# Linear attention and a two-layer MLP on one core: a new order of the first six microseconds' work on TensorE

## The chip, the cores and the metric

The kernel runs on one core of a Trainium2 chip. The metric is the device time of one launch in microseconds (us), taken as the median of several runs. The engines are TensorE (PE in the profile, PEld for its weight loads), VectorE (DVE), ScalarE (ACT), GpSimd (POOL) and SyncE (SP). Each plays its own list of instructions in order, and waits for the others by semaphores. Only PE writes products; they land in PSUM, which has 8 banks, and DVE or ACT bring them to SBUF.

## The reference

Inputs are r, k, v of shape (4 batches, 8 heads, 768 tokens, 48), a decay w and a bonus u of shape (8, 48), and two weight matrices of 384 x 2048 and 2048 x 384. Cut to what is computed:

```python
for t in range(S):                       # linear attention with a decaying state
    cur = einsum('bhd,bhe->bhde', u * k[t], v[t])
    y[t] = einsum('bhd,bhde->bhe', r[t], state + cur)
    state = w * state + einsum('bhd,bhe->bhde', k[t], v[t])
x = y.transpose(0, 2, 1, 3).reshape(3072, 384)
h = x @ w_in                             # MLP
out = maximum(0.01 * h, h) @ w_out
```

## The kernel before, in words

The tokens are cut into 24 stages of 128 (6 per batch). Within a stage the decay is split around the middle token, so that a stage's attention becomes matrix products: q~ = r times a table of powers of w, k~ = k times the inverse powers. The tables (`qtab`, `ktab`, L297 and L298) are exponentials of ln w, which is spread over all partitions by one product of a row of ones with the row w (L294) on PE and a logarithm on ACT (L296).

A stage n goes through steps, each a letter in the string ORDER (L26): **P** makes q~ and k~ on DVE (L322, L324); **T** turns both by products with an identity matrix (`ident`), in two halves of four products (L367), each half copied out of PSUM (ACT L378; the first k~ half on DVE, L375); **A** makes the scores k~ q~ (L391); **M** masks them with a triangle on DVE (L409); **X** multiplies the turned q~ and k~ on DVE (L329), and **K** makes from it the diagonal's sums and the new k v products on PE (L421, L425, L430); **Q** scales v by these sums on DVE (L337); **S** makes the next state on DVE (L475); **Y** puts the attention's output together on PE (L508, L513) with a copy on ACT (L528); **G** and **J** are the first MLP product on PE with its activation on ACT (L541 and L558), **H** the second (L575). **U** spreads u. From stage 8 on the turning is done by a DMA (L317) instead of T.

Three steps occur at the head alone. **C** (`decay_columns`, L449 and L450) makes columns of w and of w times u, by sixteen products with one column each from single rows; ACT takes the logarithm of the w columns (L457) and DVE copies the w\*u columns into `wu` (L459), which K uses. **W** (L466) makes from the logarithms the state's decay `wl` on ACT. **F**n (`fill`, L249) issues n products of 128x512 from a tile of ones (L254) whose result nobody reads. `fill(EARLY)` stands ahead of the w product (L294).

The order is written out by hand: the string ORDER is walked letter by letter, and each step appends its instructions to the lists of the engines it uses. So the order of the letters is the order on every engine. A helper records for each instruction what it reads and writes and gives it the waits that follow from that. After ORDER a loop takes the remaining stages in pairs.

POOL issues nearly all loads (L217 for r, k and v of one stage, L227 for a quarter of w_in, L231 for a quarter of w_out), in the order of the string LOADS (L25); `id` and `tri` in it are the two small tiles `ident` (L262) and `mask` (L266), made by POOL itself from the ones. r and k of stage 0 come by SP and ACT (L205), v of stage 0 is issued by POOL ahead of LOADS. The stages' loads land one after the other until about 48 us.

Of the kernel before, what the change touches and what calls it, by code (L numbers as in the profile page):

```python
# [20 lines left out]
NFB = DFF // 128  # L21
NSL = HD // 128

FIRST, EARLY = 6, 2
LOADS = """r1 k1 r2 k2 wi0 id v1 r3 tri k3 v2 wi1 k4 r4 v3 wi2 k5 r5 r6 k6 v4 v5 k7 wi3 r7 v6 v7 wo3 wo2 wo1 wo0"""  # L25
ORDER = """  # L26
C W P0 P1 F1 T0 T1 P2 A0 X0 M0 A1 K0 T2 Q0 X1 Y0 A2 S0 M1 K1 X2 G0.0 Q1 P3 S1 Y1 T3 K2 M2 G1.0 X3 A3 U G0.1 S2 G1.1 Q2 M3 Y2 K3 P4
T4 Q3 G2.0 G2.1 G0.2 S3 G2.2 G1.2 Y3 P5 A4 P6 X4 M4 T5 X5 G3.0 K4 Q4 A5 S4 T6 G3.1 K5 G3.2 Y4 M5 L8 Q5 Y5 P7 A6 G1.3 J2.0 J2.1 T7
M6 X6 X7 K6 J2.2 J2.3 A7 S6 J2.4 J2.5 L9 Q6 G2.3 G0.3 J2.6 M7 L10 J2.7 L11 G3.3 K7 S7 P8 Q7 Q8 P9 H0 Q9 K8 H1 P10 L12 K9 H2 S8 S9
Y6 Y7 A8 A9 P11 M8 H3 M9 L13  # L30
# [90 lines left out]
def bass_rwkv5_eagle__then__act_leaky_relu_kernel(  # L121
# [146 lines left out]

    for name in LOADS.split():
        if name == "id":  # L270
# [547 lines left out]
```

## Time and profile before

| what | value |
|---|---|
| time, median of 3 runs (lowest to highest) | 170.77 us (170.43 to 171.89) |
| the profiled run, its own time | 171.27 us |
| span of the profiled run, first to last instruction | 169.5 us |
| PE busy | 163.1 us, 96% of the span |
| DVE, ACT, POOL busy | 114.9, 93.3, 103.8 us |
| DVE idle from 9.79 us to 18.36 us | 0.26 and 1.14 us |
| first turning on PE | 7.30 us |
| first mask on DVE | 10.13 us |

The profile is of one execution. A group's line gives line, engine, operation, what it writes and reads, its count, busy time and mean length, and then the idle time of the engine just before such instructions. In the timeline a row gives the start from the span's begin, the length of the merged instructions, and, in brackets, how long the engine had been idle before and what ended that. PE's products are pipelined: the next starts before the one before has ended, so distances from start to start tell its speed better than lengths.

### The profile page before, as it was taken

To read this page: it belongs to the slowest core of one execution; us is meant where nothing else is said; L and a number is where in the kernel's file an instruction comes from. 1 tells how busy PE (TensorE), PEld (TensorE's weight loads), DVE (VectorE), ACT (ScalarE), POOL (GpSimd) and SP (SyncE) were. 2 spreads that over 40 slices of the span, in tenths; PEclk is the share of its full clock that TensorE was granted. 3 is DMA by queue.
4 is the path that set the end of the run, shared out by engine and by line. 5 is a ranking of instruction groups with operands and counts; after the bars stand their busy time and mean duration, and the time that the engine had idled before them with its cause. 6 is when DMAs were issued, how large, how long until landed. Compare 5 with 4: busy or idle time off the path is not lost.

```text
span 169.5 us, 5112 instructions
## 1 busy us (share of the span) xinstructions
PE 163.1 (96%) x2203; PEld 129.1 (76%) x2203; DVE 114.9 (68%) x211; ACT 93.3 (55%) x176; POOL 103.8 (61%) x117
## 2 busy tenths in 40 slices
PE   6799999999999999999999999999999999999992
PEld 1577898889656876876866867867867899898991
DVE  7699766752998869379289299099199976053272
ACT  4752888789122852842933934824834836829320
POOL 7999999990379799791992995974506500000000
PEclk9999999999999999999999999999999999999999
DMA  5999999999999989999699499599107102011032
GB/s 95 117 155 159 170 155 171 194 185 145 126 167 197 167 50 126 214 73 114 172 74 156 130 74 154 135 106 205 51 0 173 48 4 93 4 40 55 4 115 70
DMA packets 99258, 19.66 MB, mean 116 GB/s; under 512 B 92322, under 2 KB 99236, under 8 KB 99236
## 3 DMA queue, kind: packets, MB, share of 16 engines
q0 software_dynamic: 76512, 10.03, 90.9%
q1 hardware_dynamic: 21682, 9.11, 25.6%
q8 instruction: 17, 0.28, 0.7%
q10 hardware_dynamic: 1042, 0.20, 0.6%
q14 instruction: 5, 0.04, 0.1%
HBM read 20.45 MB, written 4.72 MB: 148 GB/s over the span
## 4 chain that ended last, share of the span: by engine, by line
PE 93%; POOL 4%; ACT 1%; issue 1%; DVE 0%; DVEq 0%; POOLq 0%
PE ps_all L558 31%; PE ps_all L575 25%; PE ps_all L639 11%; PE ps_all L541 7%; PE ps_all L508 7%; PE ps_all L391 4%; PE ps_all L367 3%; PE ps_all L425 3%; POOL rk_sb L217 2%; PE ps_all L513 1%; ACT tp L378 1%; POOL v_sb L217 1%; PE ps_all L430 1%; PE ps_all L421 1%; POOL w_in_sb L227 0%
## 5 line engine op out<-in xcount | busy, mean ns | idle before, releaser
L558 PE MATMUL ps_all<-xT,w_in_sb 128*128 128x256 bf16 x480 | 54.5, 273 | 0.0
L354 POOL TENSOR_TENSOR at<-ident,s_tok 128x512 bf16<-128x512 bf16 x32 | 35.0, 1121 | 29.0 <-DVE s_tok L346 29.0
L558 PEld LDWEIGHTS ps_all<-xT,w_in_sb 128*128 128x128 bf16 x480 | 46.7, 98 | 6.1
L564 ACT ACTIVATE gT<-ps_all 128x512 bf16<-128x512 f32 x80 | 47.7, 597 | 5.8 <-PE ps_all L558 1.2
L575 PE MATMUL ps_all<-w_out_sb,gT 128*128 128x384 bf16 x256 | 43.3, 326 | 0.0
L575 PEld LDWEIGHTS ps_all<-w_out_sb,gT 128*128 128x128 bf16 x256 | 24.4, 98 | 15.9
L401 DVE CAST_PREDICATED at<-mask,ps_all 128x1024 bf16<-128x1024 uint16 x16 | 18.8, 1219 | 20.6 <-PE ps_all L391 20.6
L581 ACT ACTIVATE out_sb<-ps_all 128x384 f32<-128x384 f32 x16 | 7.8, 490 | 38.4 <-PE ps_all L575 38.4
L217 POOL DMA_DIRECT2D v_sb<-in_v_dram x24 | 22.6, 945 | 0.4 <-issue 0.4
L217 POOL DMA_DIRECT2D rk_sb<-in_k_dram x23 | 21.6, 941 | 0.0
L217 POOL DMA_DIRECT2D rk_sb<-in_r_dram x23 | 21.3, 929 | 0.0
L670 DVE TENSOR_TENSOR out_sb<-ps_all,snap 128x192 f32<-128x192 f32 x13 | 4.4, 355 | 15.1 <-PE ps_all L639 14.5
L344 DVE TENSOR_TENSOR rku<-rk_sb,ku 128x384 bf16<-128x384 bf16 x16 | 13.8, 861 | 0.6
L528 ACT ACTIVATE xT<-ps_all 128x384 bf16<-128x384 f32 x24 | 11.0, 490 | 5.1 <-PE ps_all L508 3.0
L541 PE MATMUL ps_all<-xT,w_in_sb 128*128 128x128 bf16 x192 | 13.0, 225 | 0.0
L541 PEld LDWEIGHTS ps_all<-xT,w_in_sb 128*128 128x128 bf16 x192 | 11.8, 101 | 0.5 <-issue 0.3
L409 DVE TENSOR_TENSOR at<-ps_all,mask 128x512 bf16<-128x512 f32 x16 | 10.2, 682 | 2.2 <-PE ps_all L391 2.2
L546 ACT ACTIVATE gT<-ps_all 128x512 bf16<-128x512 f32 x16 | 9.6, 599 | 3.8 <-PE ps_all L541 3.1
L508 PE MATMUL ps_all<-at,v_sb 128*32 128x128 bf16 x384 | 11.4, 228 | 0.0
L378 ACT ACTIVATE tp<-ps_all 128x512 bf16<-128x512 f32 x15 | 8.2, 596 | 3.7 <-PE ps_all L367 3.7
L508 PEld LDWEIGHTS ps_all<-at,v_sb 128*32 128x32 bf16 x384 | 8.4, 99 | 2.2 <-issue 0.5
L508 PE MATMUL ps_all<-tp,st 128*32 128x128 bf16 x240 | 9.8, 223 | 0.0
(80 smaller groups left out, 197.2 us busy)
## 6 DMA issues: line engine op xcount, KB each, us to landing
out_dram<-out_sb SPq DMA_DIRECT2D x22, 192.0 KB, 2.6
v_sb<-in_v_dram POOLq DMA_DIRECT2D x24, 96.0 KB, 5.5
rk_sb<-in_r_dram POOLq DMA_DIRECT2D x23, 96.0 KB, 5.2
rk_sb<-in_k_dram POOLq DMA_DIRECT2D x23, 96.0 KB, 4.6
w_in_sb<-in_moe_w_in_dram POOLq DMA_DIRECT2D x4, 384.0 KB, 7.0
w_out_sb<-in_moe_w_out_dram POOLq DMA_DIRECT2D x4, 384.0 KB, 10.9
out_dram<-out_sb SPq DMA_DIRECT2D x4, 96.0 KB, 1.7
tp<-qk SPq DMA_TRANSPOSE x16, 4.4
```

What stands on the lines that cost most here:

```text
L217: add("pool", lambda: G.dma_start(dst, src), R=pace, W=[key], dma=f"{which}{n}")
L344: add("dve", lambda: V.tensor_tensor(rku[i2][:, :], r_of(n), ku[i2][:, :], ALU.mult), R=[("r", n % NRK), ("ku", i2)], W=[("rku", i2)])
L354: add("pool", lambda hh=hh, s_of=s_of: G.tensor_tensor(at[ia][:, hh, :, :], ident[:, :].unsqueeze(1).to_broadcast([128, NP, 128]), s_of.un ...
L401: add("dve", lambda: V.copy_predicated(at[n % NAT][:, :, :, :].rearrange("p two m i -> p (two m) i"), mask[:, :].bitcast(mybir.dt.uint16). ...
L409: add("dve", lambda hh=hh, part=part: V.tensor_tensor(at[n % NAT][:, hh, :, :], part, mask[:, :].unsqueeze(1).to_broadcast([128, NP, 128]) ...
L508: last = PE.matmul(ps_y[32 * q:32 * q + 32, 128 * s:128 * s + 128], a, m, start=first_mm and (s == 0 or n >= DIAG), stop=last_mm and n >= ...
L528: add("act", lambda: A.activation(xT[m % NX][:, :, 128 * half:128 * half + 128], ps_y[:, 0:HD].rearrange("p (s t) -> p s t", t=128), AF.Copy),
L541: last = PE.matmul(ps_g[:, 128 * f:128 * f + 128], w_in_sb[:, s, 128 * fb:128 * fb + 128], xT[ix][:, s, t], start=s == 0, stop=s == NSL - 1)
L558: last = PE.matmul(ps_g[:, 256 * f:256 * f + 256], w_in_sb[:, s, 128 * fb:128 * fb + 128], xT[ix][:, s, :], start=s == 0, stop=s == NSL - 1)
L564: add("act", lambda: A.activation(gT[ig][:, 2 * j:2 * j + 2, :].rearrange("p f t -> p (f t)"), ps_g[:, :], AF.Prelu, alpha=0.01), R=[key], ...
L575: last = PE.matmul(ps_o[:, 0:HD], gT[ig][:, s, 128 * half:128 * half + 128], w_out_sb[:, s, :], start=s == 0, stop=s == NFB - 1)
L639: done = PE.matmul(ps_o[:, 0:NH], lhs[:, s, :], rhs[:, s, :], start=first and s == 0, stop=s == HF - 1, skip_group_check=not (first and last))
```

## The change

Four things in the two strings and one constant:

- EARLY goes from 2 to 3: three dummies instead of two ahead of the w product.
- In ORDER, P0 (q~ and k~ of stage 0), a group of five dummies, P1 and the first turning T0 now come ahead of C and W; before, C and W came first, with one dummy and both turnings behind. A group of two dummies stands between W and T1. On DVE this puts q~ and k~ of stages 0 and 1, and the copy of the first turned k~, ahead of the two w\*u copies; on ACT it puts the copy of the first turned q~ ahead of the logarithms of the columns and the state's decay. On PE the sixteen one-column products move behind the first turning.
- In LOADS, `id` moves from behind the first quarter of w_in to the front: POOL makes `ident` right behind its first issue (v of stage 0), ahead of the loads of r and k of stages 1 and 2 and of w_in's first quarter.
- Everything from P2 on, and the rest of LOADS from v1 on, keeps its order.

```diff
-FIRST, EARLY = 6, 2
-LOADS = """r1 k1 r2 k2 wi0 id v1 r3 tri k3 v2 wi1 k4 r4 v3 wi2 k5 r5 r6 k6 v4 v5 k7 wi3 r7 v6 v7 wo3 wo2 wo1 wo0"""
+FIRST, EARLY = 6, 3
+LOADS = """id r1 k1 r2 k2 wi0 v1 r3 tri k3 v2 wi1 k4 r4 v3 wi2 k5 r5 r6 k6 v4 v5 k7 wi3 r7 v6 v7 wo3 wo2 wo1 wo0"""
 ORDER = """
-C W P0 P1 F1 T0 T1 P2 A0 X0 M0 A1 K0 T2 Q0 X1 Y0 A2 S0 M1 K1 X2 G0.0 Q1 P3 S1 Y1 T3 K2 M2 G1.0 X3 A3 U G0.1 S2 G1.1 Q2 M3 Y2 K3 P4
+P0 F5 P1 T0 C W F2 T1 P2 A0 X0 M0 A1 K0 T2 Q0 X1 Y0 A2 S0 M1 K1 X2 G0.0 Q1 P3 S1 Y1 T3 K2 M2 G1.0 X3 A3 U G0.1 S2 G1.1 Q2 M3 Y2 K3 P4
```

## The prediction

> **What bounds the kernel now.** I read the page first: shares, slices, and the chain that ended last.
>
> ```profile
> span 169.5 us, 5112 instructions
> ...
> PE 163.1 (96%) x2203; PEld 129.1 (76%) x2203; DVE 114.9 (68%) x211; ACT 93.3 (55%) x176; POOL 103.8 (61%) x117
> ...
> PE   6799999999999999999999999999999999999992
> ...
> PEclk9999999999999999999999999999999999999999
> ...
> PE 93%; POOL 4%; ACT 1%; issue 1%; DVE 0%; DVEq 0%; POOLq 0%
> ```
>
> TensorE (PE) is full from the second slice on and is 93% of the chain. So whatever the head wins or loses on PE by about 20 us goes straight to the end, unless something later makes PE wait. The PEclk row says full clock throughout, which the durations contradict. The timeline of the first 22 us (start, length, engine, line, out<-in, count, idle before) shows it:
>
> ```profile
> 2.61 1.64 PE L294 MATMUL ps_all<-w_row,one_row 1*128 1x384 f32 x2
> ...
> 5.66 0.61 PE L254 MATMUL ps_all<-ones 128*128 128x512 bf16 x1
> ...
> 6.16 0.35 DVE L459 CAST wu<-ps_all 48x4 bf16<-48x4 f32 x2 [1.27 <-ACT wcol L457]
> ...
> 6.54 0.56 DVE L322 TENSOR_TENSOR qk<-r_f,tab 128x384 bf16<-128x384 f32 x1
> 6.68 0.57 POOL L262 TENSOR_SCALAR_AFFINE_SELECT ident<-ones 128x128 bf16<-128x128 bf16 x1
> ...
> 7.30 1.98 PE L367 MATMUL ps_all<-ident,qk 128*128 128x128 bf16 x16 [1.04 <-POOL ident L262]
> ...
> 9.52 0.36 DVE L324 TENSOR_TENSOR qk<-rk_sb,tab 128x384 bf16<-128x384 bf16 x1 [0.19 <-DMA rk_sb<-in_k_dram]
> ...
> 9.79 0.42 DVE L329 TENSOR_TENSOR prod<-tp 128x512 bf16<-128x512 bf16 x1
> ...
> 10.99 1.05 PE L367 MATMUL ps_all<-ident,qk 128*128 128x128 bf16 x8
> ...
> 14.21 1.49 PE L541 MATMUL ps_all<-xT,w_in_sb 128*128 128x128 bf16 x12
> ...
> 14.46 0.56 DVE L337 TENSOR_TENSOR vs<-v_sb,ps_all 128x384 bf16<-128x384 bf16 x1 [0.26 <-PE ps_all L430]
> ...
> 16.65 0.61 PE L367 MATMUL ps_all<-ident,qk 128*128 128x128 bf16 x8
> ...
> 17.53 0.83 PE L541 MATMUL ps_all<-xT,w_in_sb 128*128 128x128 bf16 x12
> ...
> 18.36 0.42 DVE L329 TENSOR_TENSOR prod<-tp 128x512 bf16<-128x512 bf16 x1 [1.14 <-ACT tp L378]
> ```
>
> Three things are to be seen. Twelve L541 products take 1.49 us at 14.21 and 0.83 us at 17.53, and eight turnings 1.05 us at 10.99 and 0.61 at 16.65: up to about 16 us PE runs at half speed. VectorE (DVE) is the second full engine there: by the busy times of the stretches 8 to 16 us it works 7.37 of 8 us, PE 7.8. And at 9.52 DVE waits for the DMA that brings k of stage 2; X0 (9.79) and the mask M0 (10.13) follow at once.
>
> **The change, step by step.** All sums are against the profiled run: 171.27 us, that is the span of 169.5 and 1.8 around it. The median of the three timed runs, 170.77, is 0.5 lower.
>
> *A third early dummy.* Dummies on PE start 0.42 us apart (two in 1.03, each 0.61 long). Three from 1.65 leave PE free at 2.91; the w product, which started at 2.61, is 0.30 later. ScalarE's ln and two exponentials follow it: the q table ends at 5.79 instead of 5.49, the k table at 6.30 instead of 6.00.
>
> *The first q~ ahead of the w\*u copies.* q~0 started at 6.54, behind the copies, with its table ready at 5.49. Now it starts at 5.84 and ends at 6.40: 0.70 earlier; its r landed at 4.7 (issued 1.19, 3.5 to landing). k~0 (needs the k table) runs 6.32 to 6.96.
>
> *ident first on POOL.* It moves from 6.68 to 2.47, behind the first v load, and is done at 3.04, so it no longer holds the first turning T0 (1.04 idle at 7.30). Four load issues (r1, k1, r2, k2) and w_in's first move 0.52 us later (its slot: 6.68 to 7.20); later issues stay. Cost between 0 and 0.52. For 0 speak the landings: the first v load lands 4.5 us after issue, the next three 4.2, 4.1 and 3.9, so they queue behind each other and an issue half a microsecond later still finds its predecessor in transfer. k2 took 4.4, and wi0 6.0. I take 0; the other end is a rival below.
>
> *Five dummies to the turning.* From the w product's start to the first one-column product was 1.57 us, so F5 starts at 2.91 + 1.57 = 4.48, runs 5 x 0.42 and ends at 6.58. q~0 is ready at 6.40, so T0 starts at 6.58, not 7.30, and PE has no hole from 1.65 to T0's end at 7.43 (two halves of 0.42 from rows of half speed).
>
> *One-column products, two dummies, then T1.* These now stand between T0 and T1. At half speed: C 1.48 (4.18 to 5.66), F2 0.84, so T1 starts at 9.75 instead of 8.25. At full speed no row shows C; its bounds are 0.74 (half) and 1.48 (nothing gained), and the nearest rows, four L421 products of two columns (0.13 us to the next start at 10.58, 0.10 at 17.10), give 1.1. With T0's second half at 7.02 to 7.24 (k~0's end), C to 8.35, F2 0.43 and T1 0.45, A0 starts at 9.3, as before (9.22). The wu copies wait for C and then stand ahead of q~2 on DVE, done by about 9.1; the state's wl, behind them on ScalarE, is not used before 12.1. k~2 still waits for its load at 9.49. So **M0 stays at 10.13** and the 0.7 won on q~0 is worth nothing: the load is late next.
>
> *So all hangs on when PE becomes fast.* In the run before, PE was occupied from 1.65 to 6.27 with holes of about 0.1, but 1.5 us of this were one-column products and 1.6 the one-row product; it stayed slow. In the change 5.8 us are occupied, 1.4 of them by the one-row product, and no one-column product among them. I take it that this makes PE fast between 5 and 8 us. [...]
>
> *What a fast PE is worth.* Not half of its 7.8 busy microseconds, since DVE's work from M0 on is the same. From 9.79 to X3 (18.36) DVE idles 0.26 and 1.14, 1.40 in all: the most that can go. I follow the chain: v·s of stage 1 (L337) starts without its 0.26, ends at 14.76 instead of 15.02; Y1 starts some 0.2 later, at 14.96. From Y's start to ScalarE's copy of it: 0.88 at full speed (20.51 to 21.39), 1.22 here; from that copy, with the two copies of T3, to X3: 1.51 (16.85 to 18.36). X3 at 14.96 + 0.88 + 1.51 = 17.35, so **1.0 earlier**; ScalarE is late next. The masks M2 and M3, Y2 and the PE-bound rest follow. Later slack: r6 lands at 24.4 for an X4 at 25.0 whose mask waits 1.32 for PE; the two DMA turnings that A8 and A9 (51.63) need land at 49.8 and 50.9, which leaves 0.7, and they are issued earlier when PE is. I take the 1.0 whole: 171.27 - 1.0 = **170.3**; the bounds are 0.5 and 1.4, so 169.9 to 170.8.
>
> **Rivals.**
> - *PE isn't fast early; slower.* [...] Then the added dummies only stand in the way: A0 comes 0.97 after T1's start, at 10.72 instead of 9.22, its mask at 11.37 instead of 10.13, 1.24 late. Of A0's 1.5 the weight loads' hole of 0.47 ahead of A1 takes some. Price 1.0 to 1.24 if PE turns fast about where it did, 0.4 if earlier, up to 1.7 if later: 171.7 to 173.0, about 172.4. [...] It decides if PE is still slow at T1.
> - *The loads move.* PE is fast, but ident's 0.52 goes through to k2 (9.49 to 10.0) and the queue behind it. M0 is 0.52 late and half of the gain is gone: 170.8, to 171.3 if the DMA turnings are late as well.
> - *PE's full gain.* If DVE's order doesn't hold PE up, 7.8 us at the ratio 0.83/1.49 give back up to 3.4: 168 to 169. Against it: DVE has no hole from 9.79 to 14.2.
>
> **How the numbers follow.** The forecast 0.46 (170.3), no fast PE 0.38 (172.4), loads 0.09 (170.8), full gain 0.07 (168.5). One per cent, about what a measurement of this kernel can tell from no change, is 1.7 us: 169.06 and 172.48. Faster is the full gain, 0.07. Slower is the upper part of the second case, 0.22. The rest, 0.71, lies within. The range leaves out the full gain and the end of the second case: 169.6 to 172.9; the forecast's own is 169.9 to 170.8.
>
> **What would show it.** Eight turnings of T1 in about 0.6 us rather than 1.05; ident ending near 3.0 and q~0 near 6.4; no hole on PE up to 7.4; M0 near 10.1 and X3 near 17.4. The forecast is wrong if T1 is slow, if k2 lands near 10.0, or if PE, once fast, goes slow again in the thinner stretch behind T1.

## The result and the profile after

The changed kernel takes 172.83 us (median of 9 runs, 172.24 to 173.23), the kernel before 171.03 (9 runs, 170.43 to 171.89): a ratio of the means of 1.0098, 95% interval 1.0074 to 1.0122, so about 1.7 us slower. The forecast was 170.3. The profiled run has a span of 170.7 us instead of 169.5. One run of the experiment e8 below (174.74 us at a mean granted clock of 0.95, the others at 0.996 or more) is left out of its ratio, and its profile, which is of that run, is read up to 11 us alone, where its rows have the lengths of e7's.

The page of the changed kernel (span; busy time; slices of PE and of its granted clock; the chain by engine):

```profile
span 170.7 us, 5126 instructions
...
PE 164.3 (96%) x2210; PEld 129.0 (76%) x2210; DVE 115.1 (67%) x211; ACT 93.5 (55%) x176; POOL 104.7 (61%) x117
...
PE   6979999999999999999999999999999999999992
...
PEclk9975999999999999999999999999999999999999
...
PE 90%; POOL 3%; DMA 2%; DVE 2%; issue 1%; ACT 0%; DVEq 0%; POOLq 0%
```

PE has lost 3 points of the chain; DMA and DVE have 2 each instead of none, and POOL has 3 instead of 4. The clock row shows two low slices, 8.5 to 17 us. The timeline of the first 22 us shows what happened there:

```profile
2.49 1.49 POOL L262 TENSOR_SCALAR_AFFINE_SELECT ident<-ones 128x128 bf16<-128x128 bf16 x1
3.04 1.64 PE L294 MATMUL ps_all<-w_row,one_row 1*128 1x384 f32 x2
...
3.93 0.92 POOL L217 DMA_DIRECT2D rk_sb<-in_r_dram  x1
...
6.01 0.56 DVE L322 TENSOR_TENSOR qk<-r_f,tab 128x384 bf16<-128x384 f32 x1 [1.13 <-issue]
...
6.72 0.97 PE L367 MATMUL ps_all<-ident,qk 128*128 128x128 bf16 x8
...
8.45 0.36 DVE L324 TENSOR_TENSOR qk<-rk_sb,tab 128x384 bf16<-128x384 bf16 x1 [0.94 <-DMA rk_sb<-in_k_dram]
...
8.96 0.61 PE L367 MATMUL ps_all<-ident,qk 128*128 128x128 bf16 x8
...
10.61 0.36 DVE L324 TENSOR_TENSOR qk<-rk_sb,tab 128x384 bf16<-128x384 bf16 x1 [0.54 <-DMA rk_sb<-in_k_dram]
10.88 0.42 DVE L329 TENSOR_TENSOR prod<-tp 128x512 bf16<-128x512 bf16 x1
...
10.92 0.61 PE L391 MATMUL ps_all<-tp 48*128 48x128 bf16 x8 [1.02 <-ACT tp L378]
...
11.33 1.29 DVE L409 TENSOR_TENSOR at<-ps_all,mask 128x512 bf16<-128x512 f32 x2
...
11.87 1.05 PE L367 MATMUL ps_all<-ident,qk 128*128 128x128 bf16 x8
...
17.85 0.61 PE L367 MATMUL ps_all<-ident,qk 128*128 128x128 bf16 x8
...
19.55 0.43 DVE L329 TENSOR_TENSOR prod<-tp 128x512 bf16<-128x512 bf16 x1 [1.17 <-ACT tp L378]
```

T0 and q~0 came early, as meant, and T1 ran at full speed (0.61 for eight). But `ident` took 1.49 us, r1 was issued 1.46 later than before, DVE waited for k1 and k2, and the first mask came at 11.33 instead of 10.13. A1 waited 1.02 for T1's copies, T2 was slow again (1.05), and X3 came at 19.55 instead of 18.36. The 1.2 us of the first mask are X3's 1.2 and the span's 1.2: nothing is given back later in this run. The chain that ended last, cut to the first 22 us (start, length, what), names the beginning:

```profile
1.41 1.07 POOL v_sb L217
2.49 1.49 POOL ident L262
3.97 2.61 POOL rk_sb L217 x3
6.58 4.00 DMA rk_sb<-in_k_dram
```

The busy times by stretches (length, then busy time and instructions of PE, PEld, DVE, ACT, POOL, then the granted clock) show PE fast, slow and fast again:

```profile
core 0: us, PE busy (x) PEld busy (x) DVE busy (x) ACT busy (x) POOL busy (x), PEclk, DMA share, GB/s
...
7.50:9.00 1.50, 1.50 (x30) 1.14 (x29) 0.56 (x3) 0.83 (x3) 1.50 (x2) 1.00 2.14 111
9.00:10.80 1.80, 0.90 (x17) 0.62 (x15) 1.20 (x5) 1.74 (x4) 1.80 (x4) 1.00 1.34 111
10.90:12.00 1.10, 1.08 (x18) 0.89 (x19) 1.07 (x4) 0.00 (x0) 1.10 (x3) 0.50 1.23 183
...
16.00:17.70 1.70, 1.70 (x38) 1.31 (x36) 1.70 (x5) 0.60 (x1) 1.70 (x3) 0.50 1.91 166
17.80:20.00 2.20, 2.10 (x41) 1.82 (x39) 1.03 (x3) 1.87 (x4) 2.20 (x4) 1.00 1.97 168
```

The clock's record begins at 7.5 us with full speed, falls to half at 10.9 and rises at 17.7: 3.4 us fast, 6.8 slow. Ahead of its first record the row reads as full: in the kernel before the record begins at 16.4, and the page has 9 in every slice, also where eight turnings take 1.05 us (10.99).

Of the nine runs the mean clock is 0.98 in three (172.45, 172.83, 172.84), which is what those 6.8 slow us behind an early start make: 6.8 of 171 us at half clock. It is 0.998 or more in six (172.24 to 173.23). The mean alone does not tell when PE turned fast in those six; the profiles of e3, e12 and e6 below, which have PE's new order too, caught it at 16.5, 18.9 and 12.7. So in at least a third of the runs PE turned fast early, those are not the faster ones, and the profiled run is one of them.

### The profile page after: what moved, and what is told of

It reads as the page before. It is cut to its first block, busy times and chain, and to the rows that moved or that the text cites. A ratio compares the mean times of both kernels' runs of the same rounds, so it can differ in the third digit from the quotient of the medians.

```text
span 170.7 us, 5126 instructions
## 1 busy us (share of the span) xinstructions
PE 164.3 (96%) x2210; PEld 129.0 (76%) x2210; DVE 115.1 (67%) x211; ACT 93.5 (55%) x176; POOL 104.7 (61%) x117
## 4 chain that ended last, share of the span: by engine, by line
PE 90%; POOL 3%; DMA 2%; DVE 2%; issue 1%; ACT 0%; DVEq 0%; POOLq 0%
PE ps_all L558 31%; PE ps_all L575 25%; PE ps_all L639 11%; PE ps_all L541 7%; PE ps_all L508 7%; PE ps_all L391 4%; PE ps_all L425 3%; DMA rk_sb<-in_k_dram 2%; POOL rk_sb L217 2%; PE ps_all L367 1%; PE ps_all L513 1%; POOL ident L262 1%; DVE at L409 1%; POOL v_sb L217 1%; PE ps_all L430 1%
```

## The experiments

Two theories stood at first: L, late loads behind a slow `ident`, and P, PE's new order. Ratios are to the kernel before on the same chip, with 95% intervals; where a profile is read, it is that run's one profiled execution.

### One part at a time

**e1**, `ident` first, nothing else:

```diff
-LOADS = """r1 k1 r2 k2 wi0 id v1 ...
+LOADS = """id r1 k1 r2 k2 wi0 v1 ...
```

> The kernel before with one edit: ident first on POOL. Theory L (late loads: ident runs beside DVE's long memset, takes 1.5 us instead of 0.6, and everything that POOL issues behind it comes 1.5 us later, so that k of stage 2 lands 1.1 us later and X0 and the first mask follow): ident 1.5 us, k2 lands near 10.6, first mask near 11.3, time 1.0 to 1.4 above the kernel before. Theory P (PE's new order costs the time: one-column products and dummies between T0 and T1 on a PE that goes slow again): this kernel has PE's old order, time within 0.3 of the kernel before.

172.51 us, ratio 1.0081 (1.0055 to 1.0107). `ident` took 1.48 us, k2 landed at 11.24. The timeline:

```profile
11.26 0.36 DVE L324 TENSOR_TENSOR qk<-rk_sb,tab 128x384 bf16<-128x384 bf16 x1 [1.40 <-DMA rk_sb<-in_k_dram]
11.54 0.42 DVE L329 TENSOR_TENSOR prod<-tp 128x512 bf16<-128x512 bf16 x1
11.88 1.28 DVE L409 TENSOR_TENSOR at<-ps_all,mask 128x512 bf16<-128x512 f32 x2
```

DVE stands 1.40 us for that load (the profile is of the slowest of the four runs, 173.34). So L's part alone costs 1.4 us (0.0081 of 171), as expected.

**e2**, everything but the place of `ident`:

```diff
-LOADS = """id r1 k1 r2 k2 wi0 v1 ...
+LOADS = """r1 k1 r2 k2 id wi0 v1 ...
```

> The changed kernel with ident made behind the issue of k2 instead of first. Theory L: k2 lands near 9.5 again, the first mask at 10.1 to 10.3 where PE is fast at T1, time 0.7 below to 0.3 above the kernel before. Theory P: PE's order is that of the change, time 1.2 to 1.8 above the kernel before, first mask above 11.2.

172.54 us, ratio 1.0089 (1.0069 to 1.0109): P's time. k2 landed at 9.03 and the first mask stood at 10.40, so in this run the loss is not at the place that P had named. PE's timeline shows where it is:

```profile
9.69 0.40 PE L391 MATMUL ps_all<-tp 48*128 48x128 bf16 x8
11.11 0.52 PE L391 MATMUL ps_all<-tp 48*128 48x128 bf16 x8 [1.02 <-ACT tp L378]
11.57 0.27 PE L421 MATMUL ps_all<-wu,prod 128*128 128x2 bf16 x4
11.70 0.48 PE L425 MATMUL ps_all<-v_sb,qk 128*128 128x96 bf16 x4
11.98 1.05 PE L367 MATMUL ps_all<-ident,qk 128*128 128x128 bf16 x8
```

The same rows of the kernel before, and ACT's list in e2:

```profile
8.90 1.08 ACT L378 ACTIVATE tp<-ps_all 128x512 bf16<-128x512 f32 x2 [0.35 <-PE ps_all L367]
...
10.04 0.61 PE L391 MATMUL ps_all<-tp 48*128 48x128 bf16 x8 [0.21 <-ACT tp L378]
```

```profile
9.20 0.75 ACT L466 ACTIVATE wl<-wcol 48x192 bf16<-48x192 f32 x2
9.97 1.08 ACT L378 ACTIVATE tp<-ps_all 128x512 bf16<-128x512 f32 x2
```

A1 comes at 11.11 instead of 10.04: T1 stands behind C and F2 on PE, and ACT copies its halves behind the logarithms and wl, at 9.97 instead of 8.90. In this run too PE was fast from 7.8 to 11.2 and slow from there to 18.1. By the mean clock (0.98 in this run, 0.999 in the other three) it is the one of the four with that early start. With PE slow at T1, as in the profile of e6 below, A0 and the first mask themselves come late, where P had them. Each half of the change thus costs nearly the whole by itself, and together they cost little more. That fits two delays of the same point: K0 starts at 10.58 before, 11.46 with the change, 12.02 in e1 and 11.57 in e2.

**e4**, the changed kernel without the added dummies:

```diff
-FIRST, EARLY = 6, 3
+FIRST, EARLY = 6, 2
-P0 F5 P1 T0 C W F2 T1 P2 ...
+P0 P1 T0 C W T1 P2 ...
```

> The changed kernel without F5 and F2 and with two early dummies instead of three; its order and its early ident stay. Theory L: k2 lands near 10.6 as in the changed kernel, the first mask near 11.2, time within 0.4 of the changed kernel. Theory P: the dummies ahead of T1 are what makes A0 late, time 0.6 or more below the changed kernel. If the dummies' early full speed, where it comes, is worth something in the changed kernel, this one is 0.5 or more above it.

173.06 us, ratio 1.0114 (1.0083 to 1.0145), with a wide spread (171.50 to 173.88): within 0.4 of the changed kernel, as L had it. But in the profiled run `ident` took 0.31 us beside the same memset, k2 landed at 9.34, the first mask stood at 10.40, A1 at 11.11, and the span was 170.0. So `ident` is not slow in every run. Two of the ten runs, the profiled one (171.74) among them, are below 172 and the others at 172.8 or more; whether `ident` was slow in those eight is not shown.

**e9**, PE's new order alone: e2 with the edit of e4, without the added dummies:

```diff
-FIRST, EARLY = 6, 3
+FIRST, EARLY = 6, 2
-P0 F5 P1 T0 C W F2 T1 P2 ...
+P0 P1 T0 C W T1 P2 ...
```

> As e2 (loads on time) without F5 and F2 and with two early dummies: PE's new order alone. If the order alone makes the loss of e2 (A1 behind T1's late copies): A1 near 11.1 and time 1.2 to 1.8 above the kernel before. If the dummies have a share: time 0.5 to 1.1 above it, and what is left to e2 is the dummies'.

172.31 us, ratio 1.0060 (1.0036 to 1.0084): the order costs 1.0 us, A1 stands at 11.20. The dummies' share in e2 would be the other 0.5 us, but the intervals overlap, so that share is not shown.

**e5**, e2 with the columns behind T1:

```diff
-P0 F5 P1 T0 C W F2 T1 P2 ...
+P0 F5 P1 T0 T1 C W F2 P2 ...
```

> As e2 (loads on time), but C, W and F2 behind T1 instead of between T0 and T1. Theory A (with loads on time the loss of e2, 1.7 us, comes from T1 standing behind C and F2: its copies on ACT, and with them A1 and PE's list behind A1, are 1.0 us late): T1 starts below 8.2, its copies are done by 9.7, A1 no later than A0 allows (by 10.6), time 0.6 to 1.2 below e2. Theory K (the loss comes from PE going slow again, or staying slow, behind the first dummies): nothing is won, time within 0.4 of e2.

171.89 us, ratio 1.0040 (1.0017 to 1.0063), 0.8 below e2, so by its time the expectation held. By its profile it did not: T1 ran at 7.90, but then C and the dummies took PE to 11.3 at half speed, where A0 and A1 followed in one go. The wait moved from A1 to A0, in a run with PE slow until 16.7.

### What makes `ident` slow

**e3**, the long memset of v_sb moved behind DVE's small ones:

```diff
-    add("dve", lambda: V.memset(v_sb[...], 0.0), W=["v0"])
     add("dve", lambda: V.tensor_tensor(wu_row[:, :], w_row[:, :], u_row[:, :], ALU.mult),
...
     add("dve", lambda: V.memset(wu[:, :, :], 0.0), W=["wu"])
+    add("dve", lambda: V.memset(v_sb[...], 0.0), W=["v0"])
```

> The changed kernel with DVE's 1.34 us memset of v_sb moved behind its small memsets, so that DVE does nothing while ident is made. If ident's 1.5 us come from running beside that memset: ident 0.6 us, r1 issued near 3.0, k2 lands 9.6 to 10.0, time 0.5 to 1.2 below the changed kernel. If they are the price of this place on POOL: ident 1.5 us again and the changed kernel's time within 0.3.

172.31 us, ratio 1.0077 (1.0054 to 1.0101): 0.4 below the changed kernel, between the two expectations and within the noise of both. `ident` took 0.31, r1 was issued at 2.72, k2 landed at 10.06; PE was slow at T1 in this run, and the first mask (11.73) waited 0.87 for A0, not for k2. The short `ident` looked like the memset's doing, but e4 has 0.31 beside it. What differs between the runs is the product of the rows w and u (L286), the next in DVE's list: where `ident` took 1.5 (the changed kernel, e1) DVE had passed its wait for w at 2.28 and 2.29, before `ident` started at 2.48 to 2.49; in e4 at 2.56, just after. And `ident` ended at 3.97, 0.15 behind the product's end at 3.82. In the kernel before it ended at 7.25, 0.15 behind q~0 (7.10), which also reads two tiles.

**e12**, the product moved, the memset left:

```diff
-    add("dve", lambda: V.tensor_tensor(wu_row[:, :], w_row[:, :], u_row[:, :], ALU.mult),
-        R=["w_row", "u_row"], W=["wu_row"])
...
     add("dve", lambda: V.memset(wu[:, :, :], 0.0), W=["wu"])
+    add("dve", lambda: V.tensor_tensor(wu_row[:, :], w_row[:, :], u_row[:, :], ALU.mult),
+        R=["w_row", "u_row"], W=["wu_row"])
```

> The changed kernel with DVE's product of the rows w and u (L286, two operands in SBUF) moved behind DVE's small memsets; the long memset stays where it was, beside ident. Theory W (ident waits for that product, not for the memset: in the changed kernel and in e1 ident ends 0.15 us after the product's end at 3.82, the product having become ready at 2.28, before ident started; in e4 it became ready at 2.56, just after ident started, and ident took 0.31): ident 0.3 us in this kernel too, r1 issued at 2.7, k2 lands 0.5 to 1.3 earlier than 10.6, time 0.2 to 0.9 below the changed kernel. Theory B (the memset blocks it): ident ends no earlier than 3.4, r1 issued after that, time within 0.3 of the changed kernel.

172.16 us, ratio 1.0059 (1.0037 to 1.0080), 0.7 below the changed kernel, though the intervals just overlap. The timeline:

```profile
2.07 1.34 DVE L285 MEMSET v_sb<- 128x1536 uint32 x1 [0.27 <-issue]
...
2.48 0.31 POOL L262 TENSOR_SCALAR_AFFINE_SELECT ident<-ones 128x128 bf16<-128x128 bf16 x1
2.72 0.92 POOL L217 DMA_DIRECT2D rk_sb<-in_r_dram  x1
```

The wait for w was passed at 2.28 here as well, with the small memsets still ahead of the product, and the long memset ran all along. So neither the memset nor the landing of w held `ident`; the two-operand product did, where it was ready and next in DVE's queue (`ident` took 0.31 beside the memset here, 1.49 in the changed kernel with the product next). This is one profile for each case. k2 landed at 9.68 in this one, but PE was slow at T1 and the first mask (11.72) waited 0.88 for A0. In the changed kernel `ident` started at 2.49, 0.85 ahead of the product (3.34), and was held all the same; why is not shown.

### What holds the head, and what a fast PE is worth

**e6**, e2 with dummies in PE's wait ahead of A1:

```diff
-P0 F5 P1 T0 C W F2 T1 P2 A0 X0 M0 A1 K0 ...
+P0 F5 P1 T0 C W F2 T1 P2 A0 X0 M0 F4 A1 K0 ...
```

> As e2 with four more dummies ahead of A1, where PE idled 1.0 us in e2. Theory K: where PE turned fast early it stays fast, T2 takes 0.6 instead of 1.05, time 0.7 to 1.5 below e2 in those runs. Theory A: A1 stays at 11.1 or later, time within 0.3 of e2, up to 0.8 above it where PE is slow. If the runs in which PE turns fast early are few (three of nine in the changed kernel), the median shows Theory A's number either way, and the profile decides only if it caught such a run.

172.68 us, ratio 1.0100 (1.0071 to 1.0128): within 0.2 of e2. The profile caught no early start, so it shows the new order with PE slow at T1:

```profile
11.11 0.61 PE L391 MATMUL ps_all<-tp 48*128 48x128 bf16 x8
...
11.83 1.29 DVE L409 TENSOR_TENSOR at<-ps_all,mask 128x512 bf16<-128x512 f32 x2 [0.88 <-PE ps_all L391]
...
13.10 0.40 PE L391 MATMUL ps_all<-tp 48*128 48x128 bf16 x8
```

A0 comes at 11.11 instead of 9.22, and the first mask, at 11.83 instead of 10.13, waits for it, though k2 had landed at 9.39. PE turned fast at 12.7, 3.7 us sooner than before, but the four dummies, most of them at half speed, put A1 at 13.10, and X3 came at 19.70: no more is won by the sooner clock than the dummies ahead of it cost.

**e7**, the kernel before with the two parts that take nothing from PE:

```diff
-C W P0 P1 F1 T0 T1 P2 ...
+P0 C W P1 F1 T0 T1 P2 ...
-LOADS = """r1 k1 r2 k2 wi0 id v1 ...
+LOADS = """r1 k1 r2 k2 id wi0 v1 ...
```

> The kernel before with only the two parts that take nothing from PE: in ORDER, P0 ahead of C and W (on DVE q~0 and k~0 ahead of the w*u copies, PE's order as before), and ident behind the issue of k2. If what holds the head is k2's landing (9.5), as the prediction had it: T0 near 6.7, A1 up to 0.5 earlier, the first mask at 10.1 as before, time within 0.4 of the kernel before. If an earlier T0 carries through: 0.5 to 0.9 below it.

171.00 us, ratio 1.0000 (0.9974 to 1.0026). T0 starts at 6.35 instead of 7.30 and A1 at 9.54 instead of 10.04, but:

```profile
9.68 0.36 DVE L324 TENSOR_TENSOR qk<-rk_sb,tab 128x384 bf16<-128x384 bf16 x1 [0.99 <-DMA rk_sb<-in_k_dram]
...
9.95 0.42 DVE L329 TENSOR_TENSOR prod<-tp 128x512 bf16<-128x512 bf16 x1
10.29 1.28 DVE L409 TENSOR_TENSOR at<-ps_all,mask 128x512 bf16<-128x512 f32 x2
```

The early q~0 turns into a wait of 0.99 us for k2, as the prediction had said.

**e8**, e7 with v of stage 0 behind `ident`:

```diff
-    load_one(0, "v")
...
-LOADS = """r1 k1 r2 k2 id wi0 v1 ...
+LOADS = """r1 k1 r2 k2 id v0 wi0 v1 ...
```

> As e7, with the load of v of stage 0, which is not read before 10.6, issued behind ident instead of first, so that r and k of stages 1 and 2 are issued 1.0 us earlier. If k2's landing holds the head: k2 lands 8.5 to 8.9, the first mask at 9.3 to 9.6, time 0.4 to 0.9 below the kernel before and below e7 by as much. If not: time as e7.

170.69 us (170.55 without the run left out), ratio 0.9977 (0.9949 to 1.0005): not told from no change. k2 landed at 8.03, X0 started at 8.71 and the first mask at 9.31, as expected, but K0 then waited 0.34 for v0 and started at 10.32 instead of 10.43.

**e10**, e7 with one dummy in each of the three holes that PE has there:

```diff
-P0 C W P1 F1 T0 T1 P2 A0 X0 M0 A1 K0 ...
+P0 C W P1 F1 T0 F1 T1 P2 A0 X0 M0 F1 A1 F1 K0 ...
```

> As e7 (the kernel before with q~0 ahead of the w*u copies and ident behind k2), with one dummy each where PE idled in e7: ahead of T1, of A1 and of K0. [...] Theory N (more dummies do not move the place, or PE goes slow again in the thin stretch behind): time as e7 or up to 0.3 above.

170.06 us, ratio 0.9946 (0.9923 to 0.9969): 0.9 us faster than the kernel before, and than e7 (0.9974 to 1.0026), from which it differs by the three dummies alone. One of its twelve runs took 171.66, so not all have the gain. In the profiled run PE turned fast at 9.5 and stayed so; in the timeline all rows from A1 on are short:

```profile
9.67 0.40 PE L391 MATMUL ps_all<-tp 48*128 48x128 bf16 x8
...
10.50 0.61 PE L367 MATMUL ps_all<-ident,qk 128*128 128x128 bf16 x8
...
13.68 0.83 PE L541 MATMUL ps_all<-xT,w_in_sb 128*128 128x128 bf16 x12
...
16.88 0.42 DVE L329 TENSOR_TENSOR prod<-tp 128x512 bf16<-128x512 bf16 x1 [0.24 <-ACT tp L378]
```

X3 is 1.48 earlier than before. In this run k2 landed at 8.67, 0.8 sooner than in the profile of before, which may be a part of it.

**e11**, e10 with v of stage 0 behind k2 and `ident` behind that:

```diff
-    load_one(0, "v")
...
-LOADS = """r1 k1 r2 k2 id wi0 v1 ...
+LOADS = """r1 k1 r2 k2 v0 id wi0 v1 ...
```

> As e10, with the load of v of stage 0 behind k2 and ident behind it. [...] Theory N: as e8, 0.2 to 0.6 below the kernel before.

170.16 us, ratio 0.9937 (0.9910 to 0.9965): as e10. With PE fast from 9.8 on, k2 at 8.09 instead of 8.67 wins nothing more. By their intervals e10 and e11 are both faster than the kernel before and than the changed one.

## Why the prediction was wrong

The forecast of 170.3 took three things that did not hold: that `ident`'s move costs nothing, that A0 and A1 come no later than before, and that PE is fast from 5 to 8 us on and stays so. `ident`'s move alone costs 1.4 us (e1), and the order with its dummies alone 1.5 (e2).

*A third dummy and q~0.* The w product came 0.43 later, not 0.30; q~0 started at 6.01 and T0 at 6.72, for 5.84 and 6.58. Right in kind, a tenth or two off.

*ident's move costs 0.* This step failed first in time. It took ident's length from its old place (0.57) and the shift from its old slot (0.52), and asked nothing of what stands beside it on DVE in the new place. Ident took 1.49, the issues shifted by 1.46, and no queue of loads hides that: k1 landed 1.04 and k2 1.09 later. The rival "the loads move" had the mechanism, with 0.52 as its price; it measured 1.09 at k2 and, alone, 1.4 us (e1). On top of the new order it adds little: 1.0098 against 1.0089 in e2.

*A0 at 9.3, as before, and M0 at 10.13.* With PE fast A0 came at 9.51, near enough. What I left out is A1: T1's halves are copied by ACT, and ACT's list had the columns' logarithms and wl put ahead of them. A1 came 0.9 us late, and K0, T2 and Y0 stand behind it. With PE slow, A0 and M0 are late as well (11.11 and 11.83 in e6). The order alone costs 1.0 us (e9).

*PE is fast between 5 and 8 us.* No run behind the forecast shows the 5 to 8; they were the author's assumption. In at least three of nine runs PE turned fast early (at 7.5 in the profile). The step that failed is that 5.8 us of occupied PE suffice. In e3, with the same list on PE, it was busy all through 2.80 to 9.62, 6.82 of 6.82 us, and still slow behind that: eight turnings took 1.06 at 10.01 and 1.05 at 12.77, and the profile has it fast from 16.45 on (e6 from 12.66, e12 from 18.93). Nor does its busy time alone tell: from 9.62 to 13.04 it was busy for 3.21 us in e3. In the changed kernel's profile the clock changed at 7.47, 10.88 and 17.71, that is after 3.41 and 6.83 us. The 3.41 us ahead of the first of these (4.06 to 7.47) hold 0.6 us of the one-row product and then only dummies and T0. The two stretches of that length in e3, 2.80 to 6.21 and 6.21 to 9.62, hold 1.6 us of the one-row product and 1.5 us of one-column products. That such products do less to make PE fast than dummies is the author's estimate from these three stretches; no run shows it, nor what PE must do, and for how long, to turn fast.

*And it stays fast.* The text named this as what could make it wrong, without a price. The 3.4 us behind the turn held 0.9 us of one-column products, two dummies, T1, A0 and about 1.0 us of waiting, and PE fell back to half speed. The early start that did not last was worth nothing here: the three runs with it are no faster.

*What a fast PE is worth, 1.0.* Right in size: e10, which has it from 9.5 on and keeps it, takes 0.9 us less than the kernel before and than e7. X3 came at 16.88 for a forecast 17.35, helped perhaps by an early k2. The gain was there to be had, but not by this order.

*The rivals.* The slow end, 172.4 for no fast PE, is near the measured 172.83. Its place, A0 and then the mask, with 10.72 and 11.37, is what the profiles of e3, e12 and e6 show (A0 at 11.01 to 11.11, the mask at 11.72 to 11.83, each time held by PE). In the profiled runs of the changed kernel and of e2, where PE was fast at T1, it was not; there the loss is at k2 and at A1. No profile of the changed kernel with PE slow at T1 was taken, so how its other runs divide between these is not shown.

One slip in the text changes nothing: the one-row product is given 1.4 us where its own sum has 1.57 (2.91 to 4.48).

## What to carry to other kernels

Before a step is moved on one engine, look up what runs beside it on the others in the new place: its old length holds for its old neighbours (here `ident` on POOL beside DVE, 0.57 us in the old place and 1.49 in the new). When a chain is moved earlier, follow each thing that it pushes aside on every engine that it passes (here ACT's copies), and ask which wait is next (here a load). The dummies that were to bring PE to full speed did best in holes that it had anyway: three of them in holes won 0.9 us (e10), where three early, five in a block and two behind it won nothing (e2 against e9).

## What the runs showed that was not expected

- A GpSimd instruction of 0.31 us took 1.48 to 1.49 us where a DVE product of two SBUF tiles was next in DVE's queue and had passed its wait first, though that product itself started 0.85 us later. Whether it had depended on the row w, which was seen at 2.28 in some profiles and at 2.56 in others of kernels that are alike up to there; the other way round, DVE's q~0 took 0.71 instead of 0.56 where `ident` came first (e2).
- PE's clock went by steps of 3.4 us: full from 7.5 to 10.9, half to 17.7 (two steps) in the changed kernel, 7.8, 11.2 and 18.1 in e2. In the step ahead of the fall (7.47 to 10.88) PE was busy for 2.43 of 3.41 us; in e10, busy for 2.66 of the 3.41 us from 9.52 to 12.93, it stayed fast.
- The same load issued at the same time (k2, 5.06 or 5.07 us) landed between 8.59 (e5) and 9.65 us (e7) in the profiles of seven kernels.
- One-column products were faster with the clock at full, but less than twice: the sixteen of C took 0.89 us in the changed kernel (7.63 to 8.52) instead of 1.48 in the kernel before (4.18 to 5.66).
